# Delta rule and routed experts on one core: three shared PSUM pairs, a first routing after 16 steps, and the first pair of chunks inverted in 16x16 blocks

## The chip, the cores and the metric

The kernel runs on one core of a Trainium2 chip. Its time is device time in microseconds, from launch to end. The kernel before was run three times: 582.56, 584.33 and 584.58 us, median 584.33 us. The profile is of one further execution, which took 582.15 us; its span, from the first instruction in the trace to the last, is 580.4 us. All times in the tables and rows below are of that execution and count from the start of the span.

## What is computed

Inputs are q, k, v of shape (4 batches, 8 heads, 768 positions, 48) and a factor beta per position. The first half is a delta rule: one 48x48 state per batch and head is carried through the positions.

```python
k_n = k / (norm(k) + 1e-06)
for t in range(768):
    y[:, :, t] = q[:, :, t] @ state
    v_old = state.T @ k_n[t]
    state = state + beta[t] * outer(k_n[t], v[t] - v_old)
```

Its output, regrouped to (4, 768, 384), is the input x of the second half, eight experts of size 384 -> 1024 -> 384. `e = argmax(x @ w_gate)` when a local gate is under 0.5, otherwise the expert of the position before; so the choice runs through the positions of a batch in order. The result is

```python
out[b, s] = softmax(x @ w_gate)[e] * (relu(x @ w1[e]) @ w2[e])
```

All numbers are float32 at the edges. The expert products are made of three fp16 products of high and low halves each.

## The kernel before

**Chunks.** The 768 positions are cut into 12 chunks of 64. Two chunks make a pair, so there are six pairs. Within a chunk the delta rule becomes matrix work on 64x64 blocks: the Gram matrix of the keys and its triangular inverse. What is left of the sequence is one state that goes from chunk to chunk.

**K(n)** (L187 to L211) loads the keys and queries of chunk n with four 256 KB DMAs of 64 partitions each, forms the Gram products in four steps (one PSUM bank `pt` each), and copies each step out with two ScalarE and two VectorE instructions: the diagonal 32x32 blocks to `gt`, the off-diagonal ones to `G2`, the masked q-k products to `am`.

**T_(m)** (L212 to L253) inverts the 32x32 diagonal blocks of a pair of chunks. VectorE transposes `gt` into `L` so that each partition holds one block, finds the norms, scales, and then GpSimd (POOL) runs forward substitution on `X`: 31 steps j, each a product into `fg` (L241) and a subtraction from `X` (L242) over (31-j)*(j+1) elements. VectorE transposes the result into `TT` and `TX`. There are two buffers of `L` and `X`, one of `gt`, `TT`, `TX`.

**Tc(n)** (L254 to L276) joins two 32x32 inverses to one of 64x64: TensorE products f1 and f2 (32 products each, on two places of the array), with a ScalarE copy between, and ScalarE copies into `XT`.

**online(n)** (L278 to L331) is the sequential part: fk and fq (state times keys and queries), R (VectorE), p1 (inverse times R), `Us` (ScalarE), p3 (state update), `S` (ScalarE), p2, the two halves of y in fp16, four stores of y to DRAM (`xs`), one transposing DMA to `xt`, and lf/fg, which give the logits `lg` of the chunk's two routing steps (24 steps of 32 positions per batch in all).

**Routing and experts.** `Moe.graph` routes in two parts: part 0 after SP = 20 of the 24 steps, part 1 after the rest. Part 0 gives the first lot: 256 tokens for the first expert, gathered by GpSimd, transposed by TensorE, 72 up products and 48 down products. Part 1 gives the first expert's other 224 places; a third table (L674 to L676) gives the second expert's 496 places. The experts are sorted by their counts in part 0 and get fixed room (`CAPS`). `Moe.rest` then runs experts 3 to 8 in written order, TensorE product after TensorE product, with ScalarE and VectorE making the fp16 halves and GpSimd gathering and scattering. A loop `overflow` treats tokens over the room; with these inputs no expert has more tokens than its room, with a first part of 20 steps or of 16.

**PSUM.** Eight banks: two for the running state `Sps`, two for `kps` (fk and p1), two for `yps` (fq and p2), and two single banks `pt` that K, Tc, lf, routing and expert products take in turn. After the last chunk `kps` and `yps` serve as four banks for the expert outputs.

**Order.** Everything up to the second expert is a graph of operations (`Sched`). A list scheduler walks through it at build time with an assumed cost for each operation and emits the operations in the order of their assumed starts, so each engine's queue has a fixed order. Priority is the longest assumed way to the end, plus a boost (0.8e4 ns for the first lot). A `W` buffer pool of 15 holds keys and expert weights; nine buffers of `amp` and `xtp` join it once all of them are done with. The weights of the second expert wait for the last chunk's transposing DMA (L563, `A.lastx`).

Of the kernel before, what the change touches and what calls it, by code (L numbers as in the profile page):

```python
# [31 lines left out]
class Op:  # L32
    def __init__(s,fn,bufs,e,c):
        s.fn=fn; s.bufs=bufs; s.e=e; s.c=c if isinstance(c,dict) else {x:c for x in e}
        s.pre=set(); s.succ=[]; s.end=None; s.takes=fn.__code__.co_argcount>len(fn.__defaults__ or ())

class Sched:


    HOP=70; DMA=2000; BW=170.; LOOK=120  # L40
    def __init__(s): s.ops=[]; s.links=[]; s.wr={}; s.rd={}; s.pw={}
    def add(s,fn,r=(),w=(),p=(),claim=(),e='V',c=200,pri=0):
        bufs=list({id(x):x for x in [*r,*w,*p,*claim] if isinstance(x,Buf)}.values())
        o=Op(fn,bufs,e,c); o.boost=pri; k=lambda x:id(x) if isinstance(x,Buf) else (id(x[0]),)+x[1:] if isinstance(x,tuple) and isinstance(x[0],Buf) else x
# [13 lines left out]
    def rank(s):  # L58
        for o in s.ops:
            o.heirs=[]  # L60
            for q in o.pre: q.succ.append(o)
        for a,b in s.links: a.heirs.append(b)
        for o in reversed(s.ops):
            x=o.e[0]; own=min(60. if y=='S' else 1150. if y=='I' else o.c[y] for y in o.e)+s.lat(o,x)
            o.pri=own+max([q.pri for q in o.succ+o.heirs],default=0); o.bst=max([o.boost]+[q.bst for q in o.succ])
        for o in s.ops: o.pri+=o.bst
    def order(s):
        s.rank(); E={x:0. for x in 'VAGPS'}; dma=0.; out=[]; left={}; s.when=[]
# [3 lines left out]
        while avail:  # L72
            best=None; cand=[]
            for o in avail:
# [9 lines left out]
                if ok:  # L84
                    for x in o.e:
                        y='G' if x=='I' else x
                        cand.append((max(t,E[y]),o,x))
# [15 lines left out]
            busy=60. if x=='S' else 1150. if x=='I' else o.c[x]  # L103
            E[y]=t+busy
            if x in 'SI':
# [15 lines left out]
class Attn:  # L121
# [3 lines left out]
    NKV=3; NW=15; NAMP=6; NXT=3; NLX=2; NGT=1; NUS=2; SPLIT=(0,0,0,0,0,0)  # L125
# [33 lines left out]
    def build(s,extra=(),pre={},post=None):  # L159
# [52 lines left out]
        def T_(m):  # L212
# [21 lines left out]
            for j in range(31):  # L234
                n=31-j
                for p,(x0,x1,eng) in enumerate(((0,min(j+1,a),nc.vector),(a,j+1,nc.gpsimd))):
                    k=x1-x0
                    if k<=0: continue
# [656 lines left out]
```

## Time and profile before

| | |
|---|---|
| median of 3 runs | 584.33 us (582.56 to 584.58) |
| the profiled execution | 582.15 us, span 580.4 us |
| TensorE busy | 444.3 us, 77% |
| VectorE busy | 329.5 us, 57% |
| GpSimd busy | 286.1 us, 49% |
| ScalarE busy | 210.3 us, 36% |
| mean granted TensorE clock | 0.827 of full speed |
| DMA | 72.62 MB, mean 125 GB/s |

A busy share is an average over a kernel whose two halves differ: in the first one GpSimd runs nearly all the time, in the second TensorE does. What a row says is read within its own stretch of time. The granted clock has two levels, 1.2 and 2.4 GHz; a value between is a mean over time. Every fp32 matmul is recorded twice, so 32 products are 64 records.

### The profile page before, as it was taken

How to read it: one execution, taken by the hardware profiler on the slowest of the kernel's cores; microseconds unless marked ns; L12 is line 12 of the kernel's file. 1: busy time of each engine (PE TensorE's matmuls, PEld its weight loads, DVE VectorE, ACT ScalarE, POOL GpSimd, SP SyncE). 2: the span in 40 equal slices, each digit the busy share in tenths (PEclk: the TensorE clock that was granted, in tenths of full speed). 3: DMA queues.
4: the chain of work that ended last, by engine and by line, in shares of the span. 5: the costliest groups of instructions: out<-in, count | busy, mean ns of one | idle time of the engine just before them, and what ended most of it. 6: DMA issues, size and time to landing. Idle time of an engine off the chain costs nothing. (4 is left out here: it accounts for less than half of the span.)

```text
span 580.4 us, 18802 instructions
## 1 busy us (share of the span) xinstructions
PE 444.3 (77%) x8119; PEld 336.9 (58%) x8119; DVE 329.5 (57%) x722; ACT 210.3 (36%) x346; POOL 286.1 (49%) x492
## 2 busy tenths in 40 slices
PE   4450376888887887886853589999999999999992
PEld 3340366787787877786852358555565555555551
DVE  2764217448458468233387834943849684858550
ACT  2330344543742856435314111511506051425110
POOL 4188888888888888882001521023132232322301
PEclk9985557777986599575675599999999999999997
DMA  8992001735665365353056372451564657465300
GB/s 228 262 235 61 0 3 59 183 65 147 163 132 124 117 160 147 85 113 58 4 111 246 84 176 72 127 187 47 137 183 123 174 167 190 149 204 161 82 14 25
DMA packets 64436, 72.62 MB, mean 125 GB/s; under 512 B 42931, under 2 KB 54255, under 8 KB 64352
## 3 DMA queue, kind: packets, MB, share of 16 engines
q1 hardware_dynamic: 60800, 61.35, 41.2%
q0 software_dynamic: 3552, 10.06, 5.6%
q8 instruction: 64, 1.05, 0.8%
q14 instruction: 20, 0.16, 0.1%
HBM read 52.63 MB, written 10.05 MB: 108 GB/s over the span
## 5 line engine op out<-in xcount | busy, mean ns | idle before, releaser
L242 POOL TENSOR_TENSOR X<-X,fg 128x31 f32<-128x31 f32 (+15 forms) x186 | 110.0, 592 | 14.6
L241 POOL TENSOR_TENSOR fg<-L,X 128x31 f32<-128x31 f32 (+15 forms) x186 | 98.6, 530 | 14.6
L167 PE MATMUL pt<-W 64*64 64x128 f32 x768 | 57.2, 328 | 27.1 <-DVE gt L210 14.1
L167 PEld LDWEIGHTS pt<-W 64*64 64x64 f32 x768 | 47.8, 166 | 33.2 <-DVE gt L210 17.8
L448 PEld LDWEIGHTS <-W 128*128 128x128 f16 x432 | 43.6, 101 | 33.2 <-issue 6.9
L448 PE MATMUL pt<-kv,W 128*128 128x384 f16 (+3 forms) x288 | 61.5, 346 | 0.9 <-DVE ft L450 0.7
L450 DVE TENSOR_SCALAR ft<-pt 128x384 f32<-128x384 f32 (+6 forms) x72 | 40.1, 557 | 22.9 <-ACT W L449 14.4
L167 PE MATMUL pt<-TT,G 32*32 32x32 f32 x768 | 24.4, 229 | 32.0 <-DVE TT L249 30.9
L211 DVE TENSOR_TENSOR amp<-pt,mask 128x256 f32<-128x256 f32 x48 | 20.2, 424 | 44.2 <-ACT gt L208 27.4
L449 ACT ACTIVATE W<-pt 128x256 f16<-128x256 f32 (+4 forms) x28 | 12.2, 437 | 83.9 <-PE pt L448 78.5
L433 DVE SCALAR_TENSOR_TENSOR W<-W,W 128x768 f16<-128x768 f32 (+1 forms) x33 | 36.2, 1101 | 10.1 <-ACT W L431 10.0
L167 PEld LDWEIGHTS pt<-TT,G 32*32 32x32 f32 x768 | 22.4, 134 | 33.1 <-issue 28.9
L455 PEld LDWEIGHTS <-W 128*128 128x128 f16 (+2 forms) x272 | 27.5, 101 | 20.9 <-issue 4.6
L438 POOL DMA_INDIRECT out_dram<-y,so x9 | 11.2, 1246 | 55.2 <-DVE y L456 52.8
L436 POOL DMA_INDIRECT G<-xs,gi x25 | 26.6, 1065 | 22.3 <-PE pt L612 12.6
L449 ACT ACTIVATE xtp<-pt 128x384 f16<-128x384 f32 (+4 forms) x28 | 14.7, 526 | 56.1 <-PE pt L448 45.3
L431 ACT ACTIVATE W<-W 128x768 f16<-128x768 f32 (+1 forms) x33 | 30.2, 935 | 9.6 <-DMA W<-in_moe_w_dram 7.2
L167 PE MATMUL kps<-R,xtp 64*64 64x48 f32 x704 | 32.0, 262 | 1.7 <-issue 1.6
L167 PEld LDWEIGHTS kps<-R,xtp 64*64 64x64 f32 x704 | 30.7, 180 | 2.2 <-issue 2.0
L438 POOL DMA_INDIRECT out_dram<-kf,so x7 | 7.9, 1126 | 47.7 <-DVE kf L456 25.6
L455 PEld LDWEIGHTS <-amp 128*128 128x128 f16 (+2 forms) x224 | 22.6, 101 | 14.6 <-issue 0.9
L210 DVE SCALAR_TENSOR_TENSOR gt<-pt,ma,gt 128x128 f32<-128x128 f32 x48 | 21.4, 452 | 17.0 <-ACT G L209 9.8
(307 smaller groups left out, 934.7 us busy)
## 6 DMA issues: line engine op xcount, KB each, us to landing
W<-in_kq_dram SPq DMA_DIRECT2D x48, 256.0 KB
W<-in_moe_w_dram SPq DMA_DIRECT2D x24, 512.0 KB
W<-in_moe_w_dram SPq DMA_DIRECT2D x28, 384.0 KB
kv<-in_kv_dram SPq DMA_DIRECT2D x12, 768.0 KB
xs<-y SPq DMA_DIRECT2D x48, 96.0 KB
amp<-in_moe_w_dram SPq DMA_DIRECT2D x3, 384.0 KB
G<-xs,gi POOLq DMA_INDIRECT x25
kv<-G SPq DMA_TRANSPOSE x25
```

Source lines behind the costliest of these rows:

```text
L167: mm=lambda o,l,r,st,sp,tp:MM(o,l,r,start=st,stop=sp,skip_group_check=True,tile_position=tp)
L210: add(lambda go=go,gv=gv:nc.vector.scalar_tensor_tensor(go(),gv()[:,:,32:64],s.ma[:,1:2],go(),op0=ALU.mult,op1=ALU.add),r=[ps,"mask",key], ...
L211: add(lambda gv=gv,n0=n0:nc.vector.tensor_tensor(am.t[:,n0:n0+4,:],gv()[:,:,64:128],s.mask.unsqueeze(1).to_broadcast([128,4,64]),op=ALU.mu ...
L241: eng.tensor_tensor(tv,l[:,j,j+1:].unsqueeze(2).to_broadcast([128,n,k]),x[:,j,x0:x1].unsqueeze(1).to_broadcast([128,n,k]),op=ALU.mult)
L242: eng.tensor_tensor(x[:,j+1:,x0:x1],x[:,j+1:,x0:x1],tv,op=ALU.subtract)
L431: if e in (None,s.nc.scalar): s.nc.scalar.mul(o,i,256.0)
L433: def wlo(s,st,w,k): s.nc.vector.scalar_tensor_tensor(s.wv(w,k)[:,1],s.wst(st,k),256.0,s.wv(w,k)[:,0],op0=ALU.mult,op1=ALU.subtract)
L436: return s.nc.gpsimd.indirect_dma_start(out=x[0:m],out_offset=None,in_=s.xs[0:nt,:],in_offset=bass.IndirectOffsetOnAxis(ap=ix[0:m],axis=0) ...
L448: for k in range(3): s.nc.tensor.matmul(ps,s.wv(W[k],k)[:,a,0,128*f:128*f+128],xT[:,3*b+k,:],start=(x==0 and k==0),stop=(x==2 and k==2))
L449: def uphi(s,h,ps): s.nc.scalar.activation(h,ps,AF.Relu,scale=2.0**-6)
L450: def upt(s,t,ps): s.nc.vector.tensor_scalar(t,ps,0.0,2.0**-6,op0=ALU.max,op1=ALU.mult)
L455: s.nc.tensor.matmul(po[0:m],h(a,f)[:,c:c+m],s.wv(W[k],k)[:,b,f%2,:],start=(x==0 and f==0),stop=(x==2 and f==7))
```

## The change

The parts, as they stand in the code:

- **Blocks of the first pair.** `MODE=((16,'G'),(32,'G'),...)`: for pair 0 the substitution runs on 16x16 blocks, two side by side in each 32x32 block, 15 steps over 2*(15-j)*(j+1) elements. A new function `Mg(n)` then makes the 32x32 inverses out of them for chunks 0 and 1: 64 products, a copy, 128 products, two VectorE instructions. Pairs 1 to 5 keep their 31 steps.
- **PSUM.** `kps`, `yps` and the two `pt` become three bank pairs `pr`, one free pool from which everything takes a pair (or, as `Half`, the first bank of one). K uses one pair for each half of a chunk, Tc one pair, online two.
- **K.** Two DMAs of 128 partitions and 512 KB for a chunk in place of four of 64 partitions; two steps of 16 products on four places of the array, and two copies by ScalarE and two by VectorE for each step. `gt` has two buffers.
- **Layouts.** `gt`, `TT` and `TX` have the block as the outer and the column as the inner index; f1 and f2 work on four places of the array instead of two; fk waits for the copies into `XT`.
- **Routing.** SP = 16, so part 0 needs chunks 0 to 7 and part 1 has eight steps. The boost of the lots is 38e3 and 40e3. The second expert's weights no longer wait for the last chunk. `amp` and `xtp` buffers join `W` one by one.
- **Planner.** Other costs; TensorE's cost at either clock level; an assumed exclusion of GpSimd and some VectorE instructions (`lock`); a table of priority offsets by kind of operation and chunk (`RANK`).

```diff
-    NKV=3; NW=15; NAMP=6; NXT=3; NLX=2; NGT=1; NUS=2; SPLIT=(0,0,0,0,0,0)
+    NKV=3; NW=15; NAMP=6; NXT=3; NLX=2; NUS=2; PACE=13709.6; MODE=((16,'G'),(32,'G'),(32,'G'),(32,'G'),(32,'G'),(32,'G'))
+    RANK={'E':{-1: 2.1, 0: 13.3},
...
-        s.pt=Pool_([s.pp.tile([128,512],F32,name=f"pt{i}") for i in range(2)],"pt",True)
-        s.po=Pool_([s.yps[:,0],s.yps[:,1]],"po"); s.pk=Pool_([s.kps[:,0],s.kps[:,1]],"pk")
+        s.pr=Pool_([s.pp.tile([128,2,512],F32,name=f"pr{i}") for i in range(3)],"pr",True); s.pt=lambda:Half(s.pr)
+        s.po=Pool_([s.Sps[:,0],s.Sps[:,1]],"po")
...
-                for j in range(2): add(lambda g=g,j=j:nc.sync.dma_start(KQ[g].t[B(j)].rearrange("r a t -> r (a t)"),s.kq_[n,g,j]),p=[KQ[g]],e='S',c=196608)
+                add(lambda g=g:nc.sync.dma_start(KQ[g].t.rearrange("r a t -> r (a t)"),s.kq_[n,g]),w=[KQ[g]],e='S',c=524288)
...
+            for j in range(Bk-1):
+                n=Bk-1-j; k=j+1; b2=32//Bk; ne=n*k*b2
...
+                        tv=tmp[:,:ne].rearrange("p (z i c) -> p z i c",z=2,c=k); l,x=blk(L.t),blk(X.t); sh=[128,2,n,k]
+                        eng.tensor_tensor(tv,l[:,:,j,j+1:].unsqueeze(3).to_broadcast(sh),x[:,:,j,0:k].unsqueeze(2).to_broadcast(sh),op=ALU.mult)
+                        eng.tensor_tensor(x[:,:,j+1:,0:k],x[:,:,j+1:,0:k],tv,op=ALU.subtract)
...
+        def Mg(n):
+            def m1():
+                for x in range(16):
+                    for q in range(2):
+                        for h in range(2): o=HQ(q,h); mm(p.t[o,0,32*x:32*x+32],gt.t[o,16*cc+x,:],TT.t[o,16*cc+x,:],x==0,True,(64*q+32*h,64*q+32*h))
+            add(lambda:nc.scalar.copy(Q.t.rearrange("p n t -> p (n t)"),p.t[:,0]),r=[p],w=[Q],e='A',c=600)
+            def m2():
...
+            add(lambda:nc.vector.scalar_tensor_tensor(TT.t[:,n16,16:32],pv(0),s.mb[:,0:1],TT.t[:,n16,16:32],op0=ALU.mult,op1=ALU.add),...)
+            add(lambda:nc.vector.scalar_tensor_tensor(TX.t[:,n16,0:16],pv(1),s.mb[:,1:2],TX.t[:,n16,0:16],op0=ALU.mult,op1=ALU.add),...)
...
-                add(fk,r=[*KQ,S0],w=[pk],e='P',c=32*FT)
+                add(fk,r=[*KQ,S0],w=[pk],e='P',c=1500); S.ops[-1].pc=(1800,1130,3.07,64); S.ops[-1].pre.update(C['xt']); ok=S.ops[-1]
...
-    SP=20; LOT=256
+    SP=16; LOT=256; BOOST=(38e3,40e3)
...
-                W1=s.weights(S,A,lambda:s.reg[1],["e1"],(A.lastx,A.lastfg))
+                S.tag=('W',1); W1=s.weights(S,A,lambda:s.reg[1],["e1"]); S.tag=('R',z)
...
-        psh=rot(P(A.pt)); pso=rot(P(A.po)+P(A.pk)); pst=rot([A.Sps[:,0],A.Sps[:,1]])
+        B2=lambda i:[A.pr.tiles[i][:,z] for z in range(2)]; b=[B2(i) for i in range(3)]; q=P(A.po); psh=rot([b[0][0],b[2][0]]); pso=rot([q[0],b[1][0],q[1],b[1][1]]); pst=rot([b[0][1],b[2][1]])
```

## Rows read from the trace of the kernel before

**Rows 1.** Busy time of each engine in eight stretches, cut at the starts of the first four substitutions, at the end of the sixth, at the last logits, at the end of the first lot's products and at the last scatter. Columns: stretch, its length, busy time and count of PE, PEld, DVE, ACT, POOL, granted clock, DMA share, GB/s.

```profile
0.00:27.34 27.34, 13.03 (x160) 10.38 (x160) 13.85 (x44) 8.90 (x21) 7.58 (x58) 1.00 0.95 246
27.34:67.02 39.68, 7.44 (x96) 6.07 (x96) 18.18 (x43) 5.31 (x16) 34.82 (x63) 0.63 0.52 118
67.02:105.25 38.23, 27.81 (x720) 26.03 (x722) 19.25 (x45) 18.21 (x32) 33.37 (x62) 0.59 0.11 30
105.25:144.15 38.90, 32.94 (x1111) 31.35 (x1109) 22.75 (x52) 20.43 (x35) 34.04 (x62) 0.76 0.57 136
144.15:265.12 120.97, 97.37 (x3497) 92.08 (x3492) 63.88 (x135) 62.72 (x98) 106.46 (x186) 0.77 0.52 127
265.12:305.46 40.34, 29.58 (x1005) 28.16 (x1005) 22.73 (x78) 15.75 (x19) 1.67 (x2) 0.63 0.32 62
305.46:350.67 45.21, 25.99 (x226) 18.62 (x227) 27.91 (x91) 11.46 (x19) 13.11 (x14) 0.68 0.59 165
350.67:570.77 220.10, 210.11 (x1322) 124.17 (x1319) 140.95 (x238) 67.56 (x106) 54.07 (x46) 1.00 0.46 133
```

**Rows 2.** Timeline of GpSimd: the start of the first substitution, the starts of the first steps of the second one (31, 60, 87, 112, 135 elements), and its last instruction.

```profile
27.34 0.53 POOL L241 TENSOR_TENSOR fg<-L,X 128x31 f32<-128x31 f32 x1
...
67.02 0.24 POOL L241 TENSOR_TENSOR fg<-L,X 128x31 f32<-128x31 f32 x1
...
67.68 0.29 POOL L241 TENSOR_TENSOR fg<-L,X 128x60 f32<-128x60 f32 x1
...
68.44 0.33 POOL L241 TENSOR_TENSOR fg<-L,X 128x87 f32<-128x87 f32 x1
...
69.28 0.37 POOL L241 TENSOR_TENSOR fg<-L,X 128x112 f32<-128x112 f32 x1
...
70.24 0.42 POOL L241 TENSOR_TENSOR fg<-L,X 128x135 f32<-128x135 f32 x1
...
71.28 0.46 POOL L241 TENSOR_TENSOR fg<-L,X 128x156 f32<-128x156 f32 x1
...
264.87 0.25 POOL L242 TENSOR_TENSOR X<-X,fg 128x31 f32<-128x31 f32 x1
```

**Rows 3.** Timeline of VectorE and TensorE up to the start of the second substitution: the transposes of the first pair's `gt`, the last scaling of the second pair's `L`, and Gram products of chunks 1 and 2.

```profile
21.51 1.42 DVE L218 STREAM_TRANSPOSE L<-gt 128x256 f32<-128x256 f32 x4
...
48.46 0.68 DVE L232 TENSOR_TENSOR L<-L,mm 128x512 f32<-128x512 f32 x1
...
14.60 2.22 PE L167 MATMUL pt<-W 64*64 64x128 f32 x32 [0.71 <-DVE gt L210]
...
21.34 1.58 PE L167 MATMUL pt<-W 64*64 64x128 f32 x30 [0.49 <-DMA W<-in_kq_dram]
31.34 3.08 PE L167 MATMUL pt<-W 64*64 64x128 f32 x32 [8.41 <-DVE gt L210]
```

**Rows 4.** DMA view of the first 20 us: GB/s in 40 slices of 0.5 us. Up to 12 us keys and queries run in pieces of 64 partitions; from 12.5 to 17 us the values, in pieces of 128.

```profile
GB/s 0 0 0 0 49 328 303 262 213 246 238 205 254 221 246 213 238 221 246 229 221 230 224 267 283 430 406 406 430 406 418 418 430 418 292 256 147 229 246 229
```

**Rows 5.** Two of TensorE's groups between the start of the second substitution and the end of the sixth: Gram products, and f1.

```profile
L167 PE MATMUL pt<-W 64*64 64x128 f32 x512 | 36.8, 327 | 7.4 <-ACT G L209 6.0 <-issue 0.6 <-DVE amp L211 0.6
...
L167 PE MATMUL pt<-TT,G 32*32 32x32 f32 x640 | 20.4, 229 | 28.4 <-DVE TT L249 27.3 <-issue 1.1
```

**Rows 6.** Timeline of GpSimd and VectorE around 122 us: a subtraction of 255 elements beside a VectorE product with two inputs in SBUF, and one alone; and VectorE's group of weight halves from 144 to 265 us.

```profile
122.19 1.28 POOL L242 TENSOR_TENSOR X<-X,fg 128x255 f32<-128x255 f32 x1
...
125.76 0.68 POOL L242 TENSOR_TENSOR X<-X,fg 128x255 f32<-128x255 f32 x1
...
121.66 1.27 DVE L276 TENSOR_TENSOR kv<-kv,nT 128x768 f32<-128x768 f32 x1
...
L433 DVE SCALAR_TENSOR_TENSOR W<-W,W 128x768 f16<-128x768 f32 (+1 forms) x7 | 8.4, 1205 | 9.6 <-ACT W L431 9.6
```

**Rows 7.** Timeline after the substitution: f1 and p1 of chunk 10, p1 of chunk 11, the last y, and the last logits.

```profile
265.65 2.01 PE L167 MATMUL pt<-TT,G 32*32 32x32 f32 x64 [3.62 <-DVE TT L249]
...
275.41 3.65 PE L167 MATMUL kps<-R,xtp 64*64 64x48 f32 x64
...
290.53 3.50 PE L167 MATMUL kps<-R,xtp 64*64 64x48 f32 x64
...
298.05 0.95 DVE L313 SCALAR_TENSOR_TENSOR y<-yps,y 128x768 f16<-128x768 f32 x1
...
305.28 0.18 DVE L330 TENSOR_SCALAR lg<-lg 128x18 f32<-128x18 f32 x1
```

**Rows 8.** Around the last logits and up to dense expert products: the first gathers of the first lot and of the second expert (GpSimd); the transposes of the first lot's first tokens, its first up products and its down products (TensorE); the copy of the last of the first expert's tokens (ScalarE).

```profile
303.49 1.28 POOL L436 DMA_INDIRECT hz<-xs,gi  x1 [38.37 <-DMA xs<-y]
...
324.68 1.20 POOL L436 DMA_INDIRECT G<-xs,gi  x1 [12.63 <-PE pt L612]
...
307.94 0.82 PE L444 MATMUL pt<-mident,hz 128*128 128x128 f16 x6 [3.42 <-DVE sml L596]
...
313.66 2.08 PE L448 MATMUL pt<-W,W 128*128 128x256 f16 x9 [0.69 <-ACT W L639]
...
342.87 7.96 PE L455 MATMUL pt<-W,W 128*128 128x384 f16 x48 [1.71 <-ACT W L639]
...
342.02 0.80 ACT L639 COPY W<-pt 128x768 f16<-128x768 f16 x1 [1.78 <-PE pt L444]
```

**Rows 9.** The last scatter.

```profile
571.04 0.98 POOL L438 DMA_INDIRECT out_dram<-xt,so  x1 [3.79 <-DVEq L827]
```

More of the change, by code (lines that the diff above doesn't have):

```diff
@@ L60, in rank, with span, fill @@
             o.heirs=[]
+            o.gaps=[]
             for q in o.pre: q.succ.append(o)
         for a,b in s.links: a.heirs.append(b)
+        for a,b,d in s.gaps: a.gaps.append((b,d))
         for o in reversed(s.ops):
             x=o.e[0]; own=min(60. if y=='S' else 1150. if y=='I' else o.c[y] for y in o.e)+s.lat(o,x)
-            o.pri=own+max([q.pri for q in o.succ+o.heirs],default=0); o.bst=max([o.boost]+[q.bst for q in o.succ])
-        for o in s.ops: o.pri+=o.bst
+            o.pri=max([own+max([q.pri for q in o.succ+o.heirs],default=0)]+[q.pri+d for q,d in o.gaps]); o.bst=max([o.boost]+[q.bst for q in o.succ])
+        for o in s.ops: o.pri+=o.bst+1e3*(s.bias.get(o.tag,0)+s.bias.get(o.tag[0],0))
+    def span(s,o,t):
+        if not o.pc: return o.c['P']
+        c,w,n,q=o.pc; k=int(t//s.WIN)
+        while len(s.hot)<=k:
+            m=len(s.hot)-1; s.hot.append(s.act.get(m,0)>=(s.DN if s.hot[m] else s.UP))
+        d=w if s.hot[k] else c; a,b=s.got,s.got+q; e=t+d; s.got=b
+        for j in range(a//s.FQ,(b-1)//s.FQ+1):
+            if j>=len(s.fet): s.fet.append(max(s.fet[-1]+s.FT,s.done[j-s.FD] if j>=s.FD else 0.))
+            x=min(b,(j+1)*s.FQ); y=max(a,j*s.FQ)
+            e=max(e,s.fet[j]+d*(b-y)/q)
+            if x==(j+1)*s.FQ: s.done.append(max(t,s.fet[j])+d*(x-y)/q)
+        return e-t
+    def fill(s,o,t,d):
+        if not o.pc: return
+        a=t
+        while a<t+d-1e-3:
+            k=int(a//s.WIN); z=min(t+d,(k+1)*s.WIN+1e-3); s.act[k]=s.act.get(k,0)+o.pc[2]*(z-a)/d; a=z
     def order(s):
-        s.rank(); E={x:0. for x in 'VAGPS'}; dma=0.; out=[]; left={}; s.when=[]
+        s.hot=[False]; s.act={}; s.got=0; s.fet=[0.]; s.done=[]
+        s.rank(); E={x:0. for x in 'VAGPSL'}; dma=0.; out=[]; left={}; s.when=[]
         todo=[o for o in s.ops]
@@ L102, in order @@
             y='G' if x=='I' else x
-            busy=60. if x=='S' else 1150. if x=='I' else o.c[x]
+            busy=o.iss if x=='S' else 1150. if x=='I' else s.span(o,t) if x=='P' else o.c[x]
+            if x=='P': s.fill(o,t,busy)
             E[y]=t+busy
+            if x=='G' or (x=='V' and o.lock): E['L']=t+busy
             if x in 'SI':
@@ L684, in tokens @@
             return bd,xv
-        N=s.CAPS[1]; X1,xv1=tokens(1,"gi2"); hh=tuple(A.W() for _ in range(4)); hv=lambda a,f:f16(hh[2*a+f//4].t)[:,s.CAP*(f%4):s.CAP*(f%4)+N]
+        S.tag=('E',1); N=s.CAPS[1]; X1,xv1=tokens(1,"gi2"); hh=tuple(A.W() for _ in range(4)); hv=lambda a,f:f16(hh[2*a+f//4].t)[:,s.CAP*(f%4):s.CAP*(f%4)+N]
         for f in range(8):
```

218 lines of the change are left out of this document (127 added, 91 removed), and 13 rows, old and new, of the table RANK.

## Prediction

> **What bounds the kernel now.** I read the windows first, with cuts at the starts of the substitutions, because the page's busy shares mix two halves [rows 1]. From 27.34 to 265.12 us GpSimd is busy 35 of every 39.7 us; the rest is spread over the joints of 62 instructions, so it works without a break. From 350.67 to 570.77 TensorE is busy 210.11 of 220.10 us at a granted clock of 1.00 of full speed (the 2.4 GHz level). Between them lie two stretches in which no engine is full: 40.34 us from the last substitution to the last logits, and 45.21 us to the end of the first lot's down products. Then the timeline of GpSimd [rows 2], to see that the substitution starts at 27.34 us and that each step has its own length, and the timelines of the joints [rows 3, 7, 8], to see what each joint waits for. The page's chain of waits does not help: it holds only the last scatter. So the path is: first Gram matrices, six substitutions on GpSimd, chunks 10 and 11, routing part 1 with its gathers, expert products, last scatter. What shortens one of these five shortens the kernel, unless another engine steps in.
>
> **The change part by part**, in the time of the profiled execution.
>
> *Start, 27.34 us before.* The first pair's `gt` is complete when its transposes begin at 21.51; scaling takes the rest [rows 3]. Eight Gram steps run before, two of them (32 records) in 2.22 us, each waiting for VectorE to give a bank back. After, there are four steps with half as many copies, on three pairs. The keys came at 205 to 267 GB/s in 64-partition pieces, the values at 406 to 430 in 128-partition pieces [rows 4]: 2 MB for two chunks would take 5 us instead of 9. Four steps at 2.22 us from 4.5 us on, plus one step's copies, end near 16. Against that, the transposes now read with a stride. I take 22.5; the bounds are 27.3 (nothing gained) and 20.
>
> *First substitution, 39.68 us before.* 31 steps of 31 to 256 elements become 15 of 30, 56, 78, 96, 110, 120, 126, 128 and back. From the starts in rows 2, a step lasts 0.66 us at 31 elements, 0.76 at 60, 0.84 at 87, 0.96 at 112, 1.04 at 135. Interpolated, the eight sizes take 0.66, 0.74, 0.81, 0.88, 0.95, 0.99, 1.01, 1.02; the first seven come twice, so 12.1 + 1.0 = 13.1 us. No row shows two blocks side by side in one instruction; if they cost as two steps of half the size, 30 steps at some 0.72 us make 21.6. I take 13.1, as the rows go by elements. Saved: 26.6 us.
>
> *A new wait?* The second substitution would start at 22.5 + 13.1 = 35.6, and needs the second pair's `L`. Before, that was ready at 49.1 [rows 3] and nobody missed it until 67. Its third chunk waited 0.49 us for keys and 8.41 us for VectorE. With two `gt` buffers, faster loads and half the copies it should come some 12 us earlier. Wait: 0 to 13 us, I take 2.
>
> *Joins of 16x16 blocks.* Two chunks with 64 + 128 products each, 768 records; f1 takes 2.01 us for 64 [rows 7], so 24 us if four places of the array gain nothing, 12 if they double the rate. They lie between 36 and 75 us, beside the second substitution. TensorE was busy 7.44 of the 39.68 us of the first one and 27.81 of the 38.23 us of the second [rows 1], and chunk 0 can now begin 25 us sooner. Cost on the path: 0; without that cover it would be at most 24.
>
> *Substitutions 2 to 6, 198.10 us before.* Their instructions are the same. What comes beside them is new: the second expert's weight halves and the first lot's, both on VectorE. Rounds 2 and 3 last 38.6 us on average, 4 to 6 last 40.3 [rows 1], and in the latter lie 7 weight-half instructions [rows 6]: 5.3 us / 7 = 0.75 us each. With 4 of the second expert's 7 before the end of the sixth round, 3 us: 201.1. Bounds 0 to 11.
>
> The rows show what this is: a subtraction on GpSimd took 1.28 us beside a VectorE product with two SBUF inputs, and 0.68 us alone [rows 6]. The Trainium skill (SBUF — State Buffer, section "Who interferes with whom") states that a VectorE instruction with two SBUF inputs contends with a GpSimd instruction that reads SBUF, through a shared read interface. By it, all seven halves (1.2 us) and eight subtractions of the first lot would hold GpSimd up for about 11 us if all fell there, and the sum would be 8 us higher. The trace agrees in kind, at 0.60 us for the one case.
>
> The substitutions then end at 22.5 + 13.1 + 2 + 201.1 = 238.7, against 265.1.
>
> *Tail, 40.34 us before.* Removed: half of f1 and f2 (2.01 us for f1, rows 7) if four places of the array work at once, so 0 to 2 us for each chunk, and 0 to 2 us of copies. Added: fk of chunk 10 waits for its `XT`, where before it was done ahead of time; some 3 us. In the old tail p1 of chunk 10 began at 275.41 and p1 of chunk 11 at 290.53, both at a granted clock of 0.63 on average [rows 1, 7]; last y 299.0, logits 305.46. The first lot is now in the same queues. I take 35; bounds 30 to 45. Logits at 273.7.
>
> *Routing and first lot, 45.21 us before.* The last logits were followed by the second expert's list (first gather at 324.68, 19 us later), the first expert's last tokens (copied by 342.8), and up to 350.8 by the first lot's down products [rows 8]. In this stretch VectorE was busy 27.9 us, with the first lot and seven weight halves in it. With the first routing after chunk 7, the lot (72 up products at 2.08 / 9 us, 48 down products in 7.96 us, together 25 us) and those halves belong ahead of it. Its cover: TensorE is idle 23.6 of 121 us in rounds 4 to 6 and 10.8 in the tail [rows 1]. What is left on the path: list without other VectorE work 14 us (19 less part of it), then gather to transposed tokens: 4.5 us from gather to transposes in the first lot [rows 8], some 9 with copies and a second gather. 23 us; bounds 18 and 32. Part 1 has eight steps instead of four, perhaps 1 us, within the bounds. Dense products from 296.7.
>
> *Dense part.* 220.10 us before; the same products, two banks for up and four for down as before. I keep it: 516.8. From the last scatter's end to the end of the span 580.4 - 570.8 = 9.6 us was left [rows 1, 9], the execution adds 582.15 - 580.4 = 1.75.
>
> *Sum.* 516.8 + 9.6 + 1.75 = 528.2 us against 582.15 profiled. The median of the runs lies 2.2 us above the profiled execution; half of it is within what I can tell. I predict **529 us**.
>
> **The rivals.**
>
> *TensorE falls behind.* For: it is busy 33 of 40 us in rounds 3 to 6 [rows 1], and the first lot adds 25 us, more at the lower clock. Against: idle time there and in the gap of the routing is larger in sum; Gram products (36.8 us) and f1 (20.4 us) [rows 5] run on more places of the array. If a half of the lot lies in front of the last two chunks' p1, the tail is 13 us longer: 542.
>
> *The first lot does not come earlier.* Weights of two experts, keys and the lot share the W buffers; if the planner finds none, or logits of chunk 7 come late, the change does not do this part. Then the last stretch is 45, not 23: 551.
>
> *Slower: PSUM pairs as the bound.* Before, online had four banks of its own. After, it takes two of three pairs for most of a chunk: p1 to last y of chunk 11 alone is 8.5 us [rows 7], with fk and fq ahead some 12 to 18 of the 19.8 us of a half round; K, Tc, lf and the lot share the third, and TensorE's queue stands still behind whichever waits. The gain of 54 us is gone when a round of two chunks lasts 11 us longer (five rounds) than its substitution's 39.6. At 13 us it is 592. Against: K and Tc need that pair for about 12 us in a half round.
>
> **How the numbers follow.** Forecast 0.66, TensorE behind 0.17, lot not earlier 0.09, PSUM slower 0.05, and 0.03 that two of these add up to no change. Half a per cent (3 us) is about what a measurement of this kernel tells from no change. Faster 0.92, same 0.03, slower 0.05. Range: low end with start 20, no wait, no halves, tail 30, gap 18: 529 - 2.5 - 2 - 3 - 5 - 5 = 511, set to 508. High end takes in the first two rivals, and the doubled first substitution with a 10 us wait (529 + 8.5 + 8): 558.
>
> **What would show it.** GpSimd's first substitution with 30 instructions in about 13 us from about 22 us on, the second right behind; the sixth ending near 239; the first lot's up products before that; from the last logits to dense products 23 us; dense 220. Wrong would be gaps of many microseconds between substitutions, rounds over 45 us, or up products of the first lot after the last logits.

## The result, and the profile after

The changed kernel takes 549.69 us (median of 4 runs, 547.54 to 552.43), the kernel before beside it 583.88 us: a ratio of 0.942, 95% interval 0.937 to 0.947. The forecast of 529 us had the sign and the path right and the gain too large by 20 us; the time lies inside the range of 508 to 558. The profiled execution took 547.54 us, with a span of 545.8 us, 34.6 us less than before's.

The windows of the changed kernel, cut as in [rows 1], with the two gaps in GpSimd's work as stretches of their own (columns: stretch, length, busy time and count of PE, PEld, DVE, ACT, POOL, granted clock, DMA share, GB/s):

```profile
0.00:20.97 20.97, 9.68 (x200) 9.22 (x204) 12.26 (x37) 6.46 (x13) 8.82 (x67) 0.86 0.93 356
20.97:35.83 14.86, 2.49 (x64) 2.01 (x56) 11.77 (x29) 2.85 (x8) 12.51 (x30) 0.61 0.67 265
35.83:72.43 36.60, 24.20 (x1242) 21.59 (x1243) 12.85 (x24) 10.99 (x23) 31.82 (x62) 0.63 0.02 4
72.43:78.89 6.46, 4.67 (x254) 4.29 (x253) 5.54 (x16) 2.91 (x7) 0.00 (x0) 1.00 0.58 149
78.89:117.21 38.32, 20.06 (x841) 18.03 (x838) 20.80 (x45) 12.71 (x28) 33.46 (x62) 0.78 0.43 117
117.21:157.35 40.14, 29.35 (x1136) 27.29 (x1134) 22.52 (x44) 16.04 (x32) 34.06 (x63) 0.70 0.49 130
157.35:198.94 41.59, 31.51 (x1264) 29.59 (x1264) 21.61 (x33) 20.93 (x37) 36.81 (x62) 0.72 0.53 147
198.94:205.39 6.45, 1.96 (x67) 1.90 (x67) 6.11 (x20) 0.23 (x1) 0.00 (x2) 0.50 0.40 65
205.39:247.64 42.25, 30.97 (x1153) 28.88 (x1157) 27.42 (x64) 15.89 (x27) 37.47 (x62) 0.59 0.43 103
247.64:296.57 48.93, 37.66 (x1250) 32.84 (x1241) 29.04 (x72) 21.81 (x38) 3.17 (x4) 0.76 0.47 126
296.57:316.30 19.73, 12.65 (x171) 9.17 (x170) 15.29 (x66) 1.70 (x3) 5.42 (x8) 0.81 0.12 41
316.30:536.50 220.20, 210.06 (x1295) 123.82 (x1293) 139.76 (x237) 67.41 (x106) 64.66 (x54) 0.99 0.52 148
```

The stretches line up with the terms of the forecast (the cut at 316.30 lies 0.4 us behind the first dense product, at 315.91; from that one the routing is 19.3 us and the dense part 220.6):

| us | forecast | measured |
|---|---|---|
| start of the first substitution | 22.5 | 20.97 |
| first substitution | 13.1 | 14.86 |
| wait for the second pair's L | 2 | 0 |
| substitutions 2 to 6, without the gaps | 201.1 | 198.90 |
| gaps ahead of the third and the sixth | not in the sum | 12.91 |
| last substitution to last logits | 35 | 48.93 |
| last logits to dense products | 23 | 19.73 |
| dense products to the last scatter | 220.1 | 220.20 |
| from there to the end of the span | 9.6 | 9.3 |

So 26.8 us were lost to the forecast in two places: two waits of GpSimd that it did not have, and a tail that grew from 40.34 us [rows 1] to 48.93 where it should have shrunk. The other terms together came out 7.4 us better. The prediction had named gaps of many microseconds between substitutions as a sign of being wrong. In the timeline of GpSimd, the first gap (the bracket: idle time before, and what ended it):

```profile
72.18 0.25 POOL L291 TENSOR_TENSOR X<-X,fg 128x31 f32<-128x31 f32 x1
78.89 0.24 POOL L290 TENSOR_TENSOR fg<-L,X 128x31 f32<-128x31 f32 x1 [6.46 <-DVE L L278]
```

The third pair's `L` is late. TensorE in the 12 us before it could begin that pair's Gram products:

```profile
49.41 0.60 PE L209 MATMUL pr<-TT,gt 32*32 32x32 f32 x28 [1.80 <-issue]
...
53.14 1.52 PE L209 MATMUL pr<-Q,TX 32*32 32x16 f32 x98 [1.63 <-issue]
...
56.87 1.57 PE L209 MATMUL pr<-TX,Q 32*32 32x16 f32 x100 [1.82 <-issue]
58.37 0.92 PE L209 MATMUL pr<-W 64*64 64x128 f32 x12
```

These are the joins of the 16x16 blocks of chunk 1, and behind them, at 58.37, the first Gram product of chunk 4 (its keys had landed before 36 us; the DMA moved 4 GB/s in the stretch from 35.83 to 72.43). The second gap, 198.94 to 205.39, looks alike on GpSimd. On VectorE, each gap ends with the last instruction of the norms and, some time after it, the scaling of `L` that GpSimd waits for:

```profile
74.66 0.19 DVE L272 TENSOR_TENSOR mm<-mm,t 128x32 f32<-128x32 f32 x1
...
78.06 0.69 DVE L278 TENSOR_TENSOR L<-L,mm 128x512 f32<-128x512 f32 x1
...
202.18 0.19 DVE L272 TENSOR_TENSOR mm<-mm,t 128x32 f32<-128x32 f32 x1
...
204.56 0.68 DVE L278 TENSOR_TENSOR L<-L,mm 128x512 f32<-128x512 f32 x1
```

So each gap has two parts. The norms are late, by 2.4 us after GpSimd's last instruction in the first gap and 3.4 in the second. Then the scaling stands in VectorE's queue, 3.2 us behind `kv`, `y` and R in the first gap, and 2.2 us behind a mask product, a weight half and three small logit instructions in the second. Last, the end of the sixth substitution (GpSimd) and what VectorE did then:

```profile
247.06 0.58 POOL L291 TENSOR_TENSOR X<-X,fg 128x31 f32<-128x31 f32 x1
```

```profile
251.96 0.96 DVE L398 SCALAR_TENSOR_TENSOR y<-pr,y 128x768 f16<-128x768 f32 x1
...
253.00 1.89 DVE L302 STREAM_TRANSPOSE TT<-X 128x256 f32<-128x256 f32 x4
254.75 2.10 DVE L305 STREAM_TRANSPOSE TX<-X 128x256 f32<-128x256 f32 x4
```

The transposes into `TT` stand behind `y` of chunk 9 and the first routing's instructions: 5.4 us in which nobody reads the finished `X`. Before, f1 of chunk 10 began 0.5 us after the substitution [rows 7]; now it begins at 256.9, 9.3 us after. The other 3.9 us are the transposes themselves: f1 on four places reads `TX` too, where before it read `TT` alone, so it waits for all eight of them. TensorE from there, f1, the larger part of fk, and p1 of chunk 10:

```profile
256.91 0.27 PE L209 MATMUL pr<-TX,G 32*32 32x32 f32 x2 [4.45 <-DVE tq L703]
...
267.29 1.94 PE L209 MATMUL pr<-S,W 64*64 64x48 f32 x59 [2.14 <-issue]
...
273.92 3.65 PE L209 MATMUL pr<-R,xtp 64*64 64x48 f32 x64
```

From f1 to p1 of chunk 10 it takes 17.0 us, 9.8 before [rows 7]; from that p1 to the last logits 22.7 us, 30.1 before. So the whole growth of the tail lies ahead of p1. The first lot's up products run from 277.5 to 294.7, in this tail and not before the end of the sixth substitution, where the prediction had them; its down products end at 304.5, after the last logits.

### The profile page after: what moved, and what is told of

Read it like the earlier page. It is cut to its first block, busy times and chain, and to the rows that moved or that the text cites. A ratio compares the mean times of both kernels' runs of the same rounds, so it can differ in the third digit from the quotient of the medians.

```text
span 545.8 us, 20203 instructions
## 1 busy us (share of the span) xinstructions
PE 415.3 (76%) x8887; PEld 308.6 (57%) x8887; DVE 325.0 (60%) x674; ACT 179.9 (33%) x323; POOL 269.2 (49%) x473
## 5 line engine op out<-in xcount | busy, mean ns | idle before, releaser
L533 PE MATMUL pr<-kv,W 128*128 128x384 f16 (+3 forms) x264 | 56.5, 343 | 3.4 <-DVE tx L807 1.9
L533 PEld LDWEIGHTS <-W 128*128 128x128 f16 x408 | 40.3, 100 | 27.6 <-issue 5.1
L535 DVE TENSOR_SCALAR gf<-pr 128x384 f32<-128x384 f32 (+6 forms) x72 | 40.1, 557 | 26.0 <-ACT amp L534 7.1
L209 PE MATMUL pr<-S,W 64*64 64x48 f32 x1408 | 36.7, 264 | 20.7 <-DVE amp L255 9.7
L209 PE MATMUL pr<-W 64*64 64x128 f32 x768 | 36.6, 346 | 17.4 <-DVE kc L481 6.1
L209 PEld LDWEIGHTS pr<-S,W 64*64 64x64 f32 x1408 | 33.6, 178 | 23.1 <-issue 12.5
L540 PEld LDWEIGHTS <-W 128*128 128x128 f16 (+4 forms) x308 | 31.3, 102 | 19.4 <-ACT W L534 1.1
L209 PEld LDWEIGHTS pr<-W 64*64 64x64 f32 x768 | 31.2, 179 | 19.5 <-DVE kc L481 6.4
L209 PE MATMUL pr<-R,xtp 64*64 64x48 f32 x704 | 32.3, 263 | 12.5 <-DVE R L372 11.8
L209 PEld LDWEIGHTS pr<-R,xtp 64*64 64x64 f32 x704 | 31.2, 180 | 13.2 <-DVE R L372 12.2
L534 ACT ACTIVATE W<-pr 128x384 f16<-128x384 f32 (+5 forms) x36 | 17.6, 489 | 36.0 <-PE pr L533 28.9
L533 PE MATMUL pr<-kv,amp 128*128 128x496 f16 (+1 forms) x96 | 27.7, 362 | 0.2 <-DVE gf L535 0.2
```

The source lines that it names most:

```text
L209: mm=lambda o,l,r,st,sp,tp:MM(o,l,r,start=st,stop=sp,skip_group_check=True,tile_position=tp)
L533: for k in range(3): s.nc.tensor.matmul(ps,s.wv(W[k],k)[:,a,0,128*f:128*f+128],xT[:,3*b+k,:],start=(x==0 and k==0),stop=(x==2 and k==2))
L534: def uphi(s,h,ps): s.nc.scalar.activation(h,ps,AF.Relu,scale=2.0**-6)
L535: def upt(s,t,ps): s.nc.vector.tensor_scalar(t,ps,0.0,2.0**-6,op0=ALU.max,op1=ALU.mult)
L540: s.nc.tensor.matmul(po[0:m],h(a,f)[:,c:c+m],s.wv(W[k],k)[:,b,f%2,:],start=(x==0 and f==0),stop=(x==2 and f==7))
```

## The experiments

Each is the changed kernel with one edit, run beside the kernel before on the same chip; the ratio is to that, and to be held against 0.942. Executions of one kernel differ by 3 to 9 us. The planner turns any edit into a new order, unless it is said that the order stays; so a difference between two runs can hold an effect of the order too. Where the table `RANK` is "fitted anew", a random search over its entries took the order with the shortest planned time.

**Is the first lot in the way of the tail?** The rival that TensorE falls behind. The order stays; the lot's operations do nothing.

```diff
             for o_ in S.ops[i_:]:
                 o_.boost=s.BOOST[z]
+                if z==0: o_.fn,o_.takes=(lambda:None),False
```

> All 25 us of the first lot's work (gathers, transposes, 72 up products, their copies, 48 down products, scatters) are left out, everything else keeps its place in every queue; 256 rows of the output are not written. Theory A, the lot lies in the way of chunks 10 and 11: the stretch from the last substitution to the last logits falls from 48.9 us to 42 or less and the time by 6 us or more, to 543 or less. Theory B, the lot fills idle time of TensorE and something else makes that stretch long: stretch 46 us or more, time 547 to 551.

Ratio 0.9384 (0.9345 to 0.9422): the same within the intervals. VectorE's first transposes into `TT` and the last logits of this run:

```profile
253.00 1.03 DVE L302 STREAM_TRANSPOSE TT<-X 128x256 f32<-128x256 f32 x2
...
296.05 0.17 DVE L415 TENSOR_SCALAR lg<-lg 128x18 f32<-128x18 f32 x1
```

From `TT` to the last logits it takes 43.2 us, with the lot 43.6; from the last substitution (245.61) 50.6. The lot is hidden in sum, as forecast, and the long tail has another cause: theory B holds. It is a sum of two effects, though. Without the lot p1 of chunk 10 comes 3.3 us sooner after f1, and from there to the logits it takes 2.9 us longer, at a granted clock of 0.70 against 0.91 with the lot's products in between.

**Transposes ahead of y.** The planner is told that the sixth substitution is shorter, and puts its transposes first.

```diff
+        for o in s.ops:
+            if o.tag==('S',5): o.c={'G':0.85*o.c['G']}
```

> The planner takes the sixth substitution for 15% shorter, so that its transposes stand on VectorE ahead of y of chunk 9. Theory A, the end of the substitution is not seen because the transposes queue behind y: TT starts within 2 us of the last GpSimd instruction instead of 5.4, and the last logits and the time come 3 to 5 us earlier (545 to 547). Theory B, the chain through TensorE and the three PSUM pairs sets the last logits: TT starts earlier, but the time stays within 1.5 us of 549.7.

Ratio 0.9335 (0.9301 to 0.937). VectorE:

```profile
245.33 1.94 DVE L304 STREAM_TRANSPOSE TT<-X 128x256 f32<-128x256 f32 x4
...
288.98 0.17 DVE L417 TENSOR_SCALAR lg<-lg 128x18 f32<-128x18 f32 x1
```

TensorE, the start of f1 of chunk 10:

```profile
249.32 0.22 PE L211 MATMUL pr<-TX,G 32*32 32x32 f32 x2 [2.53 <-DVE TX L307]
```

The transposes now begin before the substitution has ended (246.57), on the rows that are done, and the last logits come 7.4 us earlier, 43.8 us after `TT` as before. f1 waits for `TX`, 4.0 us after the start of `TT`, here too. The median over the kernel before is 5 us better than the ratio 0.942 gives; theory A holds, somewhat above its 3 to 5 us at the logits.

**fk of chunk 10 ahead of its joined inverse.** In the change, fk waits for the copies into `XT`.

```diff
+        for o in s.ops:
+            if o.tag in (('O',10),) and o.fn.__name__=='fk':
+                for q in list(o.pre):
+                    if q.tag[0]=='F': o.pre.remove(q); q.succ.remove(o)
```

> fk of chunk 10 no longer waits for that chunk's joined inverse in the plan, so it stands on TensorE right behind chunk 9. Theory A, that wait is what lengthened the stretch after the last substitution: p1 of chunk 10 starts within 20 us of the last GpSimd instruction instead of 26, time 541 to 545. Theory B, fk then holds a PSUM pair that the joins need: p1 of chunk 10 comes no earlier, time 549 to 556.

Ratio 0.9382 (0.9332 to 0.9432). VectorE:

```profile
253.65 0.95 DVE L402 SCALAR_TENSOR_TENSOR y<-pr,y 128x768 f16<-128x768 f32 x1
254.52 1.94 DVE L306 STREAM_TRANSPOSE TT<-X 128x256 f32<-128x256 f32 x4
...
291.70 0.17 DVE L419 TENSOR_SCALAR lg<-lg 128x18 f32<-128x18 f32 x1
```

p1 of chunk 10 begins at 262.48, 17.0 us after the last GpSimd instruction instead of 26.3. From `TT` to p1 it takes 8.0 us instead of 20.9, but from `TT` to the last logits 37.4 us instead of 43.6: in this order the wait costs 6 us at the logits, where I had put 3. (`TT` still stands behind y.) The time hardly moves all the same. The first lot's down products come after the last logits, and the dense products begin 23.0 us after those instead of 19.3. Mechanism as in theory A, time (547.8 us when scaled to the kernel before of the first comparison) in neither band for sure.

**Scaling of L free in the plan.** The planner had kept it off GpSimd's steps, and so behind other work.

```diff
+        for o in s.ops:
+            if o.tag[0]=='T': o.lock=0
```

> The planner no longer keeps the scaling of L away from GpSimd's steps, so it may stand on VectorE as soon as the norms are there. Theory A, GpSimd's two gaps of 6.5 us come from what stands ahead of the scaling in VectorE's queue: each gap falls to 3 to 4 us, the last substitution ends 5 to 7 us earlier, and the time falls by 3 to 7 us (543 to 547). Theory B, the gaps close but the chain of chunks behind sets the last logits: last substitution earlier, time 548.5 to 551. Theory C, the gaps come from late Gram products: both stay above 5 us.

Ratio 0.9416 (0.9351 to 0.9481): no gain. GpSimd, around the sixth pair and within the second substitution:

```profile
197.87 0.25 POOL L293 TENSOR_TENSOR X<-X,fg 128x31 f32<-128x31 f32 x1
199.37 0.53 POOL L292 TENSOR_TENSOR fg<-L,X 128x31 f32<-128x31 f32 x1 [1.25 <-DVE X L279]
```

```profile
68.27 0.45 POOL L293 TENSOR_TENSOR X<-X,fg 128x135 f32<-128x135 f32 x1
73.94 0.76 POOL L279 COPY X<-mm 128x32 f32<-128x32 f32 x1 [5.22 <-DVE mm L274]
```

The second gap was a matter of the planned order: it falls from 6.45 to 1.25 us. In the new order the scaling follows the norms at once, and the norms are there at 198.4, 4.0 us earlier than before. The first gap does not go away. The plan put the copy of the third pair's norms on GpSimd, where it waits 5.2 us in the middle of the second substitution, for norms that are ready hardly earlier than before (73.9 us; 74.9 in the changed kernel). And though the sixth substitution ended 2.9 us earlier, `TT` still began at 253.20, behind y of chunk 9: theory B for the time.

**Joins twice.** The order stays; the products that join chunk 1's blocks are issued twice.

```diff
+            if n==1: m1=twice(m1)
             add(m1,r=[gt,TT],w=[p],claim=[Q],e='P',c=1950)
...
+            if n==1: m2=twice(m2)
             add(m2,r=[Q,TX],w=[(p,1)],claim=[p],e='P',c=3000)
```

> The products that join the 16x16 blocks of chunk 1 are issued twice, with the same result; the plan and every queue's order stay as they are. Theory A, these joins hold TensorE while the third pair's Gram matrices and their G2 buffers wait, and so make GpSimd's gap ahead of the third substitution: the gap grows from 6.5 us by the doubled work, to 12 us or more. Theory B, the joins lie beside the second substitution and cost nothing, as forecast: the gap stays within 1.5 us of 6.5, and the time within 1.5 us of the changed kernel's (ratio to the kernel before 0.942).

Ratio 0.9583 (0.9508 to 0.9658), some 9 us longer. GpSimd:

```profile
72.45 0.25 POOL L291 TENSOR_TENSOR X<-X,fg 128x31 f32<-128x31 f32 x1
88.99 0.24 POOL L290 TENSOR_TENSOR fg<-L,X 128x31 f32<-128x31 f32 x1 [16.30 <-DVE L L278]
```

The gap grows by 9.8 us, all of it in norms that come later (85.2 us instead of 74.9). The joins lie on the path: theory A.

**Four parts undone.** First the blocks (`MODE` with 32 for the first pair), `RANK` fitted anew:

> The first pair's substitution runs on 32x32 blocks again, without joins of 16x16 blocks; the table of priorities is fitted anew to this graph by a search with the planner. Theory A, the account by parts holds: the first round is 24.8 us longer and the gap of 6.5 us ahead of the third substitution is gone, time 15 to 20 us longer, ratio to the kernel before 0.967 to 0.977. Theory B, what the first round gains is mostly given back later by the chain of chunks: under 8 us longer, ratio below 0.956.

Ratio 0.9779 (0.9739 to 0.9819), 0.036 above the changed kernel's, 21 us. Its windows for the first substitution and substitutions 2 to 6, cut at the second one's first subtraction, 0.3 us after it begins:

```profile
21.35:59.96 38.61, 2.54 (x79) 2.06 (x72) 13.26 (x30) 3.79 (x10) 33.67 (x65) 0.59 0.27 107
59.96:265.65 205.69, 127.48 (x5301) 118.24 (x5301) 114.58 (x225) 79.97 (x154) 177.33 (x311) 0.72 0.40 106
```

From start to start the first round is 23.4 us longer, and rounds 2 to 6 are 5.8 us shorter than 211.81 (the five rounds with both gaps): without joins the first gap is gone. Theory A, though the ratio lies a little above its band. The rounds make 17.6 of the 18.8 us between the two profiled executions.

Then the first routing, `SP=20`, `RANK` fitted anew:

> The first routing takes 20 steps again, with the other parts as changed and the table of priorities fitted anew. Theory A, the shorter stretch from the last logits to the dense products comes from the earlier routing: about 20 us longer, ratio to the kernel before 0.97 or more. Theory B, it comes from the second expert's weights, which no longer wait for the last chunk, and from the lot's higher priority: 10 us longer or less, ratio 0.96 or less.

Ratio 0.9635 (0.9575 to 0.9695), 12.5 us longer: between the two. Its windows from the last logits to the dense products, and the dense part:

```profile
299.06:322.88 23.82, 17.01 (x244) 12.87 (x242) 20.74 (x77) 6.18 (x11) 7.22 (x10) 0.84 0.28 93
322.88:548.21 225.33, 211.83 (x1296) 124.77 (x1295) 140.69 (x241) 67.59 (x106) 59.88 (x52) 0.99 0.51 144
```

From first product to first product, the stretch after the last logits is 4.5 us longer than with 16 steps, the dense part 4.7 us. Of the 25.5 us by which that stretch fell from 45.21 [rows 1], SP accounts for a small part only: with 20 steps it is still 23.8 us.

The second expert's weights, held back again until the last chunk's logits:

```diff
-                W1=s.weights(S,A,lambda:s.reg[1],["e1"])
+                W1=s.weights(S,A,lambda:s.reg[1],["e1"],(A.lastx,A.lastfg))
```

> The second expert's weights wait for the last chunk's transposing DMA and logits again, as in the kernel before; nothing else. Theory A, their earlier arrival is a large part of the shorter stretch after the last logits: 6 us longer or more, ratio to the kernel before 0.952 or more. Theory B, they are hidden by the routing: within 2 us, ratio 0.939 to 0.946.

Ratio 0.9452 (0.9383 to 0.9521). The value lies in theory B's band; the interval reaches into A's, so the times do not decide. The profiled execution is the slowest of the four (556.19 us, the fastest 547.51), so it is a hint only: the stretch after the last logits lasts 28.4 us in it, 9.0 more than in the changed kernel, and from `TT` to the last logits it takes 39.2 us, 4.3 less. The seven weight halves that stood in the latter now stand in the former. The lot's higher boost was not tried by itself; what made the rest of the 25.5 us stays open.

The table of offsets, emptied (`RANK={}`):

> The table of priority offsets is emptied, nothing else. Theory A, the gain needs the fitted order: 10 us longer or more, ratio to the kernel before 0.959 or more. Theory B, the parts carry it, and the order is worth less than 4 us: ratio below 0.949.

Ratio 0.9517 (0.9468 to 0.9566), some 6 us longer, between the bands: the parts carry most of the gain.

**A plan with GpSimd's measured speed.** The plan gave a 32x32 round 40 to 43 us between starts; the rounds in the trace last 36.6 to 42.3 without the gaps. A plan that thinks GpSimd slow lets `L` come late.

```diff
+            if o.tag[0]=='S': o.c={'G':0.9*o.c['G']}
+            if o.tag[0]=='T': o.lock=0
...
-            add(lambda e:e.tensor_copy(X.t[:,0:1024:33],mu.t),...,e='VG',c=dict(V=460,G=300))
+            add(lambda e:e.tensor_copy(X.t[:,0:1024:33],mu.t),...,e='V',c=dict(V=460,G=300))
```

With it the cut at fk from above, and `RANK` fitted anew.

> The planner gets GpSimd's steps at 0.9 of its assumed cost, the scaling of L free of the exclusion, the copy of the diagonal on VectorE, and fk of chunk 10 free of its joined inverse; the table of priorities is fitted anew. Theory A, L is late because the plan let it come just in time for a slower GpSimd, and the tail starts late because the transposes queue behind y: the gap ahead of the sixth substitution falls under 2 us, TT starts within 2 us of the last GpSimd instruction, the last logits come 8 us earlier or more, ratio to the kernel before 0.925 to 0.933. The gap ahead of the third substitution stays (4 to 7 us), because chunk 5's Gram matrices still wait for the joins through G2. Theory B, the chain of chunks on TensorE has no room: ratio 0.938 or more.

Ratio 0.9252 (0.9211 to 0.9293), the best of all, 1.8% under the changed kernel. Windows from the end of the sixth substitution on, and VectorE there:

```profile
239.52:251.13 11.61, 8.55 (x410) 7.75 (x405) 2.89 (x6) 2.41 (x3) 3.75 (x3) 0.97 0.59 135
251.13:288.99 37.86, 28.44 (x944) 25.20 (x944) 21.97 (x44) 22.02 (x38) 0.00 (x0) 0.82 0.54 146
```

```profile
248.27 0.96 DVE L406 SCALAR_TENSOR_TENSOR y<-pr,y 128x768 f16<-128x768 f32 x1 [8.14 <-ACT y L405]
...
251.13 1.90 DVE L310 STREAM_TRANSPOSE TT<-X 128x256 f32<-128x256 f32 x4
```

The gaps are 3.3 and 1.0 us; the substitutions end 8.1 us earlier than in the changed kernel. The gap ahead of the sixth and the time are as theory A says. Three points are not: `TT` comes 11.6 us after the end, not 2, behind y of chunk 9 once more, for which VectorE waits 8.1 us; the last logits come 7.6 us earlier, not 8; and the gap ahead of the third substitution falls to 3.3, under the 4 to 7 expected. There the norms are no earlier (75.4 us), but the scaling follows them at once: what is gone is the 3.2 us in VectorE's queue, what stays is the joins' part.

**Six G2 buffers.** As e9, with `s.G2=P(6,...)` and `NW=14`. Chunk 5's Gram matrices need a G2 buffer that f1 of chunk 1 must have read, and f1 follows the joins.

> As e9_replan, with six G2 buffers in place of four (and 14 W buffers in place of 15, to make room), so that the Gram matrices of chunks 4 and 5 no longer wait until f1 of chunks 0 and 1 has read G2, which follows the joins. Theory A, the joins cost time through these buffers: the gap ahead of the third substitution falls under 1.5 us and the third substitution starts at 74 us or before (78.9 in the changed kernel). Theory B, Gram products are late for another reason: the gap stays above 4 us.

GpSimd, at the third pair and the sixth:

```profile
73.25 0.25 POOL L299 TENSOR_TENSOR X<-X,fg 128x31 f32<-128x31 f32 x1
73.58 0.24 POOL L298 TENSOR_TENSOR fg<-L,X 128x31 f32<-128x31 f32 x1
...
204.49 0.24 POOL L298 TENSOR_TENSOR fg<-L,X 128x31 f32<-128x31 f32 x1 [6.05 <-DVE nT L282]
```

The first gap is gone (0.08 us instead of e9's 3.3), as theory A says. In this order the Gram products of chunks 4 and 5 run ahead of the joins, so the way through G2 is shown. But in this order gaps of 7.0 and 6.1 us open ahead of the fifth and the sixth substitution, and the ratio is 0.9344 (0.9304 to 0.9383), worse than e9. Whether the missing W buffer or the order opens them was not tried.

**The tail once more.** As e9, with factors 0.85 and, for the sixth substitution, 0.75.

> As e9_replan, with GpSimd's steps at 0.85 of the assumed cost and the sixth substitution's at 0.75, so that its transposes stand ahead of y of chunk 9 and f1 of chunk 10 gets a PSUM pair that chunk 9 does not hold; priorities fitted anew. Theory A, what is left of the late tail in e9 is the 11.6 us that TT waited in VectorE's queue: TT starts within 2 us of the last GpSimd instruction, the last logits come 4 us earlier or more than in e9 (285 us or before), ratio to the kernel before 0.911 to 0.921. Theory B, the chain of chunks 8 to 11 on TensorE sets the last logits, whatever is ahead of it: TT earlier, but logits within 2.5 us of e9's 289, ratio 0.921 to 0.931.

Ratio 0.9316 (0.9281 to 0.9351). VectorE, and TensorE's waits in the first 87 us of the dense part (columns: us in total, times, longest):

```profile
241.62 0.61 DVE L310 STREAM_TRANSPOSE TT<-X 128x256 f32<-128x256 f32 x1 [2.09 <-POOL X L299]
...
284.21 0.17 DVE L423 TENSOR_SCALAR lg<-lg 128x18 f32<-128x18 f32 x1
```

```profile
PE Sps L548 <- DVE kf L549: 5.6, 5, 2.2
PE pr L541 <- DVE gf L543: 2.2, 1, 2.2
```

`TT` follows the substitution at once, and the last logits come 4.6 us earlier than in e9, as theory A says. The time is no better: from the start of the dense products to the last scatter it takes 224.0 us against e9's 220.6, and TensorE waits longer there for VectorE's copies out of PSUM (7.8 us in these two rows, 2.5 in e9). Its ratio lies in neither band. What is won before the logits is given back behind them; why the copies come later was not tried.

## Why the prediction was right or wrong

**Right.** The path was the one named, and work by work the large terms held: the start (four Gram steps, and keys at 356 GB/s in the first 21 us against 246 [rows 1]); the first substitution by elements, not by steps (a step of 128 elements lasts 1.01 us, 1.02 interpolated from [rows 2]; the 1.8 us above forecast are mostly three instructions that ran long beside VectorE, as 1.03 us for one of 30 elements); no wait for the second pair; the dense part; the first lot hidden in sum (e1). Undoing the blocks costs 21 us (e6), near the 26.6 of the forecast less the gap that they opened.

**Right in size, not for the reason given.** The stretch from the last logits to dense products took 19.7 us for 23. I put its fall down to the first routing after chunk 7. With 20 steps it is 23.8 (e7), so that is worth 4 to 5 us there, and the rest has another cause, in part perhaps the second expert's weights (e11). That the size fitted is luck.

**Substitutions 2 to 6.** Without the gaps they took 198.90 us, 198.10 before [rows 1], so the 3 us for weight halves did not fall due: six halves lie beside rounds 5 and 6 and one in the gap between them, as many as before [rows 6], and seven more came after, in the tail. By the Trainium skill's rule (SBUF — State Buffer, section "Who interferes with whom") I had estimated up to 11 us there, if the second expert's halves and part of the lot fell beside the rounds; they did not, so the sum does not test it. In kind the trace agrees with the rule: the round with 12.85 us of VectorE beside it lasted 36.60 us, that with 27.42 us 42.25.

**Wrong: "Joins of 16x16 blocks. Cost on the path: 0."** I looked for cover beside the second substitution, in TensorE's idle time, and there was enough. What I did not follow is who waits behind the joins. Chunk 5's Gram matrices need a G2 buffer, the buffer needs f1 of chunk 1, f1 needs the joins; from there the way goes through norms and scaling to the third pair's `L`. Before, 32x32 blocks had no such step. That the joins are on the path is shown from both sides: doubled joins add 9.8 us to the gap (e5), two more buffers remove what e9 leaves of it (e10). Their cost is some 3.3 of the 6.46 us, which is what e9 leaves; the other 3.2 us are VectorE's queue between the norms and the scaling.

**Wrong: "A new wait? ... I take 2".** I bounded that wait for the second pair only. Each of the five joints can have it. The one ahead of the sixth pair, 6.45 us, comes of the planned order: norms 3.4 us late, then 2.2 us in VectorE's queue. Other orders have 1.25 us (e4, which frees the scaling) and 1.0 us (e9, which also gives GpSimd a shorter cost). That the planner's cost for GpSimd made it, rather than the order as such, is argued and not shown by itself.

**Wrong: "Tail, 40.34 us before ... I take 35".** 13.9 us too short, and what was lost lies ahead of p1 of chunk 10. From the end of the substitution to f1 it took 9.3 us (0.5 before): 5.4 us for the transposes behind y of chunk 9, not in my list, since in the kernel before they stood right behind the substitution (e2 takes them away and gains), and 3.4 us more because f1 now waits for `TX` as well, a term that I put at nothing. From f1 to p1 it took 17.0 us (9.8 before). There lies fk behind `XT`: 6 us at the logits, not 3 (e3). There too TensorE stood for 4.2 us without a named wait, where before it had no such stop. The 35 needs 8.3 us of gain from f1, f2 and copies (40.3 + 3 - 35), all that my terms allow or more. f1 of chunk 10 occupies 256.91 to 259.25, 2.3 us, against 2.01 [rows 7]. 58 of its 64 records come in the first 1.06 us, so four places were faster; two stops, of 0.18 and 0.48 us, took that back. From p1 to the last logits it was 7.4 us shorter than before, which I had not forecast: the granted clock was 0.91 there, 0.67 before, with the lot's products in between. No run changes only the clock.

**The range.** Its high end does not follow from its terms: 529 + 8.5 + 8 is 545.5, and the first two rivals give 542 and 551. (Five rounds of 13 us more make 594, too, not 592.) The measured 549.69 lies above the former, so it is the second rival's 551, which did not come true, that covers it.

**The rivals.** TensorE behind with the first lot (542 us) gave about the right size for the tail by a wrong mechanism: without the lot the tail is as long (e1). PSUM pairs as the bound did not come; the rounds last 36.6 to 42.3 us. Whether the pairs decide where fk and f1 can stand was not tried by itself.

## What to carry to other kernels

When a stage on the path gets shorter, list everything that must be ready by its new end, for every repetition of the stage and not only the next one, and follow each through the buffers that its producers wait for: work with plenty of idle time beside it is still on the path if a buffer is handed on behind it. An order made from assumed costs is just in time for those costs; measure the stage, put its duration into the plan, and look at what stands ahead of the first instruction after it in each in-order queue. And check whether time won ahead of a joint survives it: in e3, e4 and e12 it did not.

## What the runs showed of the hardware

In the joins TensorE came to a stop after every 128 matmul records, without waiting for anything that the waits name. A window of the changed kernel from the end of one such stop to the end of the next (the stretches before and behind it, 45.70 to 49.41 and 53.14 to 56.86, are alike to 0.01 us):

```profile
49.41:53.13 3.72, 2.10 (x128) 1.88 (x128) 0.00 (x0) 1.57 (x3) 3.33 (x6) 0.50 0.02 4
```

From 49.41 to 53.14, the DMA queues (queue and kind: packets, MB, share):

```profile
q8 instruction: 1, 0.02, 2.0%
```

So 128 matmuls and 128 weight loads take about 2 us of work and 3.72 us of time, 29 ns a record, at a granted clock of 0.50, and one packet of instructions is fetched in that time; in each of the two stretches beside it there is one too. Over the whole execution this queue has 70 packets, and TensorE 8887 matmuls and as many weight loads: 254 instructions a packet. The Trainium skill (Runtime: NRT & Kernel Launch, section "Instruction fetch mechanics") says that an engine's instructions are refilled in blocks of 256 and that crossing a block is mostly hidden. The trace agrees on the block; hidden it is not here, with 1.6 to 1.8 us of stop in each. That the stop is the wait for the next block is the likely reading, and no run here tries it.

The pace is that of f1 on two places before (64 records in 2.01 us, 31 ns [rows 7], at a granted clock of 0.50). At the same clock f1 of chunk 10 on four places ran 58 records in 1.06 us, 18 ns each, before its two stops; another f1 elsewhere ran its 64 records in 0.91 us (184.97 to 185.88), at a granted clock of 1.00. So packing small products on more places helped a short burst, and a long run of them fell back to the old pace. Up to the last logits TensorE's Gram, join and state products stood idle for 28.5 us with the releaser "issue", in 28 places; in the kernel before it was 8.5 us, in 11.

VectorE's four transposes into `L` took 2.10 to 2.14 us with the new layout of `gt`, 1.42 before [rows 3]: 0.7 us more for each pair, on the way to every `L`. The read with a stride is the likely cause: in the kernel before, a transpose of `X` into `TT`, read in order, took 0.40 us (median of 24), and one into `TX`, of the same size but read with a stride, 0.57.
